# Moving one row of a modulation gradient into the last stage, its products to ScalarE, and a few gradient products to other places

## The chip, the cores and the metric

The kernel runs on one core of a Trainium2 chip. The time is device time in microseconds (us) from the start of the program to its end, outputs written. Three runs before took 1404.22, 1406.06 and 1412.09 us (median 1406.06).

## What is computed

One transformer-like block and its gradient, in bf16, for S = 2048 tokens of D = 1024 features and an MLP width of F = 3584. Cut to what matters:

```python
mod = (silu(c) @ w_mod)              # six rows of 1024: sa, ca, ga, sb, cb, gb
h = layernorm(x) * (1 + ca) + sa
x = x + ga * irfft2(rfft2(h) * (w_r + 1j * w_i))
h = layernorm(x) * (1 + cb) + sb
out = x + gb * (gelu(h @ w1 + b1) @ w2 + b2)
# returned: out, and the gradients of x, w_r, w_i, w1, b1, w2, b2, c and w_mod for grad_out
```

The Fourier transforms are done as matrix products with cosine and sine matrices. The gradient of `w_mod` is an outer product of u = silu(c) (1024 values) with the gradient of `mod` (6 rows of 1024), so it is 1024 x 6144. The gradient of `c` needs, for each of the six rows, `w_mod[:, row] * gradient row` summed along the row.

## The kernel before

The kernel keeps TensorE (PE) fed with large products of 16 matmuls (128x512 each, accumulated in one PSUM tile). Two families of such products are independent of almost everything else and are used as filling between the steps of the backward Fourier transform: 56 **gw2 products** (gradient of w2, line 1289, copied out of PSUM by ScalarE, line 1297, or by any engine in the first eight blocks) and 56 **gw1 products** (gradient of w1, line 1550, copied out by ScalarE at line 1554). `pieces()` is a Python generator that emits one product for each step; `fill(n)` (line 1562) emits the next n. Both families take their PSUM tile from a pool of four (`ps_f`), so PE can be at most four products ahead of the copies.

Each engine executes its own list of instructions in order. A scheduler makes these lists when the kernel is built, from the order in which the Python code issues the operations, from priorities (`tc.high_priority()` around the copies out of PSUM) and from `tc.issue_after(ins)`, which puts what is issued under it behind the instruction `ins`. DMAs are issued by SP (plain loads, stores and transposing loads), by POOL (scattered loads and stores, the stores of the gradients of w1 and w_mod) and by ScalarE's queue (the store of each late gw2 half row, line 1298). A queue that waits to issue one DMA also holds those behind it.

The stages from about 975 us on, which the change touches:

- **Pair stage** (`spectral_core(False, ...)`, the eight steps of the loop over `par` and `m`). Each step multiplies a slice of the transform by the filter and makes the filter's gradient (VectorE, DVE, line 195), with four gw2 products as filling (`beside_bwd`, line 1589). The transposed `hh` operand of each gw2 block is loaded by SP (lines 1507 and 1509) into a ring of three buffers. Between the products `beside_bwd` also runs 17 steps of `gmod_ring` (line 1185) for **rows 3 and 4** of w_mod: SP loads 256 KB of w_mod (line 1190), DVE multiplies and sums it (line 1201), DVE makes the product `u * gradient row` (line 1203) and POOL stores it (line 1204). The steps are given out as 2, 3, 3, 3, 3, 3, 0, 0 to the eight pairs. Two inverse transforms (`s_inv`, line 652, copied out to `V` by ScalarE) come before the seventh pair.
- **Split inverse**: for the classes CO and SO `half_class` (line 1422) makes the inverse in halves (line 1431), with one `fill(1)` behind CO; then 24 small groups `po` (line 775) for four blocks of tokens, with `fill(1)` at some places of the loop over `npp` (line 765).
- **Token blocks**: `consume_bwd` (line 1460) is called for i = 0 to 3. It undoes the folds on DVE, normalizes on ScalarE (line 518), runs `scaled_rows` (line 1252) and `ln_bwd` (line 1242: a product and sum on DVE at line 1244, a scaled copy on ScalarE at line 1246, an addition on DVE), loads `d_gx1` (line 1476), adds and stores with `store_tok` (line 165 on SP, the scattered half at line 167 on POOL). It fills with 3, 7, 7, 8 products, then column sums on PE (`accCA`), then 2, 2, 1, 2.
- **Last stage** (line 1608): `gmod_row` for rows 5, 2, 1, 0. Each of its eight steps (`gmod_steps`, line 1172) loads 256 KB of w_mod on SP into a ring of four (`wrw`, line 1176), makes the product on DVE into a ring of four (part of `otl`, line 1177), stores it from POOL (line 1178) and multiplies and sums on DVE (line 1179). Beside it run the remaining 27 gw1 products, six behind each row.

Of the kernel before, what the change touches and what calls it, by code (L numbers as in the profile page):

```python
# [13 lines left out]
ACT = mybir.ActivationFunctionType  # L14
ALU = mybir.AluOpType
# [20 lines left out]
def kernel(  # L36
# [24 lines left out]
    nc = tc.nc  # L61
    CE, CO, SE, SO = 0, 1, 2, 3
# [131 lines left out]
    def tt(out, a, b, op):  # L194
        return nc.vector.tensor_tensor(out=out, in0=a, in1=b, op=op)  # L195
# [188 lines left out]
    for j in range(4):  # L384
        for cch in range(NDC):
            pt = ps_f("pt")
            for a in range(4):
                q = (0, 2, 3, 1)[a] if j % 2 == 0 else (1, 3, 2, 0)[a]
# [159 lines left out]
    def spectral_core(fwd, fb, sms, em, css, pt, evac_u, evac_c, evac_v, consume, o4tag, pfs=None, fill=lambda n: None, mid=lambda: None, beside=lambda n, r_in: None):  # L548
# [156 lines left out]
        for par in range(2):  # L705
            for m in range(4):
# [14 lines left out]
                if par == 0 and m > 0:  # L721
# [6 lines left out]
                    else:  # L728
                        cl = (CE, SE)[m - 2]
# [4 lines left out]
        for cl in (CO, SO):  # L734
            if fwd:
                s_inv_half(cl, smis[1], 0)
                continue
            Vs[cl] = reg.tile([P, 8, 512], BF16, name=f"V{cl}", tag=f"uv{cl}")

            def r_cols(c8, i, cl=cl):  # L740
                dc = c8 // 2
                base = (0, 1, 2, 1)[dc] + 256 * (c8 % 2) + (PW if (dc >= 2) == (cl < 2) else 0)
                return R[:, cl * 4 + i, :, :].rearrange("p x w -> p (x w)")[:, base:base + 255:2]

            half_class(cl, Vs[cl], r_cols, evac_v)
            if cl == CO:
                fill(1)
        with tc.issue_after(r_in[0].ins):
            nc.vector.tensor_scalar(out=gm[:, 8:12, :], in0=gm[:, 4:8, :], scalar1=-1.0, scalar2=None, op0=ALU.mult)
        xts = [reg.tile([P, 4, D], BF16, name="xt", tag="sma")[:]]  # L750
# [6 lines left out]
        for i in range(4):  # L757
            if fwd and i == 0:
                tmp, eb, o4 = first
            else:  # L760
                o4, on, tmp = ct[:, 3 * (i % 2)], ct[:, 3 - 3 * (i % 2)], ct[:, 1 + i % 2]
                if fwd and i == 2:
                    eb = tmp
            half = [(cl, eb[:, 2 * k + cl // 2], k * 256 + i // 2 * P) for cl in (CE, SE) for k in range(2)]
            for npp, (cl, ov4, c0) in enumerate((half if i % 2 == 0 else []) + [(cl, o4[:, cl], i * P) for cl in (CO, SO)]):
                if npp in (2, 4):
                    fill(1)
                for hh_ in range(2):
                    npo[0] += 1
                    po = ((ps_d, ps_s) if fwd else (ps_d, ps_s, ps_d, ps_f))[npo[0] % (2 if fwd else 4)]("po")  # L770
                    for d2 in range(2):
                        dc = 2 * hh_ + d2
                        for h in range(2):
                            gi = 2 * dc + h + (4 if (dc >= 2 and cl >= 2) else 0)
                            nc.tensor.matmul(po[:, d2 * 256:(d2 + 1) * 256], lhsT=Vs[cl][:, 2 * dc + h, c0:c0 + P],
                                             rhs=gm[:, gi, :], start=(h == 0), stop=(h == 1))
                    with tc.high_priority():
                        ov = ov4[:, hh_ * 512:(hh_ + 1) * 512]
                        if fwd or (cl, hh_) != (3, 0):
                            nc.any.tensor_copy(out=ov, in_=po[:])  # L780
                        else:
                            last_po[0] = nc.scalar.copy(out=ov, in_=po[:])
            if i % 2 == 0:
                tt(o4[:, 0:4:2, :], eb[:, 0:2, :], eb[:, 2:4, :], ALU.add)
                if fwd and i == 2:
                    tt(on[:, 0:4:2, :], eb[:, 0:2, :], eb[:, 2:4, :], ALU.subtract)
            elif not fwd or i == 1:
                tt(o4[:, 0:4:2, :], eb[:, 0:2, :], eb[:, 2:4, :], ALU.subtract)
            if i == 0:
                if fwd:  # L790
                    for cl in (CO, SO):
                        s_inv_half(cl, smis[1], 1)
                    ct = reg.tile([P, 4, 4, D], BF16, name="ct", tag=o4tag)
                xts.append(reg.tile([P, 4, D], BF16, name="xt", tag="smb" if fwd else "px0")[:])
            consume(i, o4, tmp, ct[:, 2 - i % 2], xts[i % 2], eb)
# [376 lines left out]
    def gmod_steps(r, wrs, gws, gr):  # L1172
        nc.sync.dma_start(out=gr, in_=d_gmod[r * D:(r + 1) * D].partition_broadcast(P))
        for jc in range(NDC):
            wr, gw = wrs[:, jc % wrs.shape[1], :], gws[:, jc % gws.shape[1], :]
            nc.sync.dma_start(out=wr, in_=w_mod[jc * P:(jc + 1) * P, r * D:(r + 1) * D])
            nc.vector.tensor_scalar(out=gw, in0=gr, scalar1=u_rt[:, jc:jc + 1], scalar2=None, op0=ALU.mult)
            nc.gpsimd.dma_start(out=out_9[jc * P:(jc + 1) * P, r * D:(r + 1) * D], in_=gw)
            nc.vector.tensor_tensor_reduce(out=wr, in0=wr, in1=gr, scale=1.0, scalar=0.0,
                                           op0=ALU.mult, op1=ALU.add, accum_out=gu[:, r, jc:jc + 1])  # L1180
            yield
# [57 lines left out]
    def ln_sums(gs):  # L1239
        nc.vector.tensor_scalar(out=gs, in0=gs, scalar1=-1.0 / D, scalar2=None, op0=ALU.mult)  # L1240

    def ln_bwd(g, gsum, n_ap, tmp):
        sc = small.tile([P, 1], FP32, tag="lbsc", bufs=4)
        nc.vector.tensor_tensor_reduce(out=tmp, in0=g, in1=n_ap, scale=-1.0 / D, scalar=0.0,  # L1244
                                       op0=ALU.mult, op1=ALU.add, accum_out=sc[:])
        nc.scalar.activation(out=tmp, in_=n_ap, func=ACT.Identity, scale=sc[:], bias=gsum)  # L1246
        tt(g, g, tmp, ALU.add)

    def scaled_rows(out4, in4, row, gs, r, b):
# [201 lines left out]
    sacc = otl[:, 2 * NT * P:2 * NT * P + D]  # L1451
# [8 lines left out]
    def consume_bwd(i, o4, tmp, tmp2, n1, eb):  # L1460
        if i == 0:
            accCA.append(ps_s("accCA"))
            nc.vector.tensor_copy(out=sacc, in_=eb[:, 0, :])
        elif i == 2:
            tt(sacc, sacc, eb[:, 0, :], ALU.add)
        unfold_d(o4, tmp)
        unfold_tok(o4, tmp)
        load_tok(n1, A_x, i, nc.gpsimd)
        with tc.issue_after(last_po[0].ins):
            norm_act(n1, n1, 0, i)  # L1470
        tt(tmp, o4, n1, ALU.mult)
        s1c = small.tile([P, 4], FP32, tag="s1c")
        scaled_rows(o4, o4, opca_row, s1c, 0, i)
        for q in range(4):
            ln_bwd(o4[:, q, :], s1c[:, q:q + 1], n1[:, q, :], tmp2[:, q, :])
        nc.sync.dma_start(out=n1, in_=chunk_rows(d_gx1, i))
        tt(o4, o4, n1, ALU.add)
        store_tok(out_1, o4, i)
        fill((3, 7, 7, 8)[i])
        halves_sum(accCA[0], tmp, i == 0, i == 3)  # L1480
        fill(1 if i == 2 else 2)
        if i == 3:
            rows = small.tile([P, D], BF16, tag="gmrow", bufs=1)
            store_halves(accCA[0], rows[0:64, 0:KH], tmp, 1)
# [13 lines left out]

    def gmod_row(r, ins):
        with tc.issue_after(ins.ins):  # L1500
            for _ in gmod_steps(r, w1g["wr"], w1g["gw"], w1g["gr"][:, r % 2, :]):
                pass

    def pieces():
# [36 lines left out]
        for fg in range(F // 512):  # L1541
            if fg == 3:
                w1g["gz"] += [reg.tile([P, 8, 512], BF16, name=f"gzu{k}", tag=f"uv{k}") for k in range(4)]
            for k in {0: (1,), 1: (2,), 2: (3,), 3: (4, 5, 6)}.get(fg, ()):
                w1g["ins"] = gw1_load(k)
            gz2 = w1g["gz"][2 * w1g["set"][fg]:2 * w1g["set"][fg] + 2]
            for cch in range(NDC):
                acc = ps_f("gw1acc")
                for t in range(NT):
                    nc.tensor.matmul(acc[:], lhsT=n3ns[t // 4][:, t % 4, cch * P:(cch + 1) * P], rhs=gz2[t // 8][:, t % 8, :],  # L1550
                                     start=(t == 0), stop=(t == NT - 1))
                ob = gwo1[:, (fg * NDC + cch) % 8]
                with tc.high_priority():
                    nc.scalar.copy(out=ob, in_=acc[:])  # L1554
                eng = nc.sync if fg == 6 and cch > 4 else nc.gpsimd
                eng.dma_start(out=out_4[cch * P:(cch + 1) * P, fg * 512:(fg + 1) * 512], in_=ob)  # L1556
                yield
# [4 lines left out]
    def fill(n):  # L1562
        for _ in range(n):
            next(todo)
        done[0] += n
# [18 lines left out]
        for step in step_in[3:8]:  # L1584
            behind(step, ins)

    rows34 = gmod_ring((3, 4), gmy, sacc)

    def beside_bwd(n, r_in):
        for k in range(4):  # L1590
            fill(1)
            if 3 - k < (2, 3, 3, 3, 3, 3, 0, 0)[n]:
                with tc.issue_after(hh_in[0].ins), tc.issue_after(r_in.ins) if n == 7 else ExitStack():
                    next(rows34)

    spectral_core(False, fbuf2, (smA2, None), em2, [css2[:, 0], css2[:, 1]],
                  new_pair_temps(["t0", "t1", "t2", "t3"]), s_copy, s_copy, s_copy, consume_bwd, "fr", pfs, fill, mid_bwd, beside_bwd)
# [7 lines left out]
    unfold_d(sr[0:1, 0], sr[0:1, 1])  # L1605
    store_gmod([sr[0:1, 0, 0, 0:KH], sr[0:1, 0, 0, KH:D]], 0)

    for r in (5, 2, 1, 0):
        gmod_row(r, w1g["ins"])
        fill(6)  # L1610
    fill(NFC * 4 - done[0])
    fin2 = reg.tile([P, 2, P], BF16, name="fin2", tag="gm")
    make_identity(nc, fin2[:, 0, :])
# [40 lines left out]
```

## Time and profile before

| | us |
|---|---|
| runs: lowest, median, highest | 1404.22, 1406.06, 1412.09 |
| the profiled execution's own time | 1412.43 |
| its span, first to last instruction | 1410.7 |
| TensorE busy in it | 1354.3 |
| VectorE busy | 1066.7 |
| ScalarE busy | 759.4 |

The profile is of one execution. An engine's busy time says how long its instructions ran; a row of a timeline gives start, length, engine, line and operation, `out<-in` by the program's names, how many instructions were merged (x16), and in brackets how long the engine sat idle before it and what ended that wait. PE is TensorE's matmul row, DVE is VectorE, ACT ScalarE, POOL GpSimd, SPq and ACTq the queues that issue DMAs. L1550 is line 1550 of the kernel before.

### The profile page before, as it was taken

What the parts mean: (1) busy time and instruction counts of PE and PEld (TensorE: products, weight loads), DVE (VectorE), ACT (ScalarE), POOL (GpSimd) and SP (SyncE); (2) the same over time, 40 slices, a digit from 0 to 9 for tenths busy, and PEclk for the clock granted to TensorE, in tenths of its full rate; (3) what the DMA queues carried; (4) which work ended last, traced back from release to release, by engine and by line L of the source; (5) the groups of instructions that cost most, each with busy time, mean ns of one, the idle gap of its engine ahead of it and who ended that gap; (6) DMA issues with size and microseconds to landing.
All of it is one profiled execution on the core that took longest, in us unless ns stands there. A gap on an engine that the chain in (4) does not pass through costs nothing. (4 is left out here: it accounts for less than half of the span.)

```text
span 1410.7 us, 18467 instructions
## 1 busy us (share of the span) xinstructions
PE 1354.3 (96%) x6774; PEld 658.6 (47%) x6899; DVE 1066.7 (76%) x1479; ACT 759.4 (54%) x1082; POOL 355.4 (25%) x434
## 2 busy tenths in 40 slices
PE   5898999999999999999999999999999899999998
PEld 2445565444444444444444444444644455444444
DVE  5897889977888787887620678889686778968781
ACT  4775657657967766665314593443622454534311
POOL 5410523201212122112211011011254420322542
PEclk8999999999999999999999999999999999999999
DMA  9972746799787777696999499995499987798993
GB/s 318 282 235 61 199 138 194 253 294 351 255 253 230 235 239 243 192 296 224 287 276 272 119 255 308 257 263 148 123 287 262 262 195 204 218 257 171 282 338 111
DMA packets 360689, 331.12 MB, mean 235 GB/s; under 512 B 207962, under 2 KB 303088, under 8 KB 360470
## 3 DMA queue, kind: packets, MB, share of 16 engines
q1 hardware_dynamic: 319702, 204.96, 55.8%
q0 software_dynamic: 35136, 119.73, 24.1%
q10 hardware_dynamic: 5760, 5.25, 1.2%
q8 instruction: 54, 0.88, 0.3%
q14 instruction: 37, 0.30, 0.1%
HBM read 165.73 MB, written 114.87 MB: 199 GB/s over the span
## 5 line engine op out<-in xcount | busy, mean ns | idle before, releaser
L840 PE MATMUL pp<-gBoT,wt 128*128 128x512 bf16 x874 | 196.5, 380 | 4.3 <-ACT phr L846 1.9
L1131 PE MATMUL pg<-w1T,gzr 128*128 128x512 bf16 x877 | 194.3, 379 | 1.3 <-issue 0.5
L1550 PE MATMUL gw1acc<-gzh,n3n 128*128 128x512 bf16 x627 | 139.1, 379 | 3.8 <-ACT gwo L1554 3.1
L1550 PEld LDWEIGHTS <-n3n 128*128 128x128 bf16 x896 | 87.4, 98 | 108.7 <-issue 5.0
L840 PEld LDWEIGHTS <-wt 128*128 128x128 bf16 x896 | 87.6, 98 | 107.9 <-issue 6.4
L1131 PEld LDWEIGHTS <-gzr 128*128 128x128 bf16 x896 | 86.6, 98 | 108.4 <-issue 5.8
L977 PEld LDWEIGHTS <-w 128*128 128x128 bf16 x896 | 87.2, 98 | 106.9 <-issue 2.5
L977 PE MATMUL pz<-n3Tb,w 128*128 128x512 bf16 x437 | 98.4, 379 | 1.7 <-DVE w2sD L1053 1.0
L977 PE MATMUL pz<-n3Ta,w 128*128 128x512 bf16 x439 | 98.0, 379 | 0.4
L1289 PE MATMUL gw2acc<-gB,hhsA 128*128 128x512 bf16 x405 | 93.1, 384 | 5.1 <-DMA hhsA<-d_hhT 4.5
L195 DVE TENSOR_TENSOR ct<-ct 128x2048 bf16<-128x2048 bf16 (+1 forms) x84 | 91.5, 1117 | 7.6 <-DMA d_n<-ct 3.7
L1031 PEld LDWEIGHTS <-hhA 128*128 128x128 bf16 x608 | 59.0, 98 | 72.8 <-issue 2.6
L980 ACT ACTIVATE gt<-pz,b_col 128x512 bf16<-128x512 f32 x112 | 72.8, 683 | 33.3 <-PE pz L977 33.0
L988 ACT ACTIVATE gt<-gt 128x2048 bf16<-128x2048 bf16 x28 | 53.5, 1911 | 64.5 <-DVE gt L195 64.5
L1554 ACT CAST gwo<-gw1acc 128x512 bf16<-128x512 f32 x56 | 31.9, 582 | 98.5 <-PE gw1acc L1550 70.9
L195 DVE TENSOR_TENSOR gt<-gt,gt 128x2048 bf16<-128x2048 bf16 x56 | 68.5, 1224 | 19.8 <-ACT gt L990 18.5
L1297 ACT CAST gwo<-gw2acc 128x512 bf16<-128x512 f32 x40 | 23.5, 586 | 96.0 <-PE gw2acc L1289 72.7
L1289 PEld LDWEIGHTS <-hhsA 128*128 128x128 bf16 x416 | 40.8, 99 | 53.7 <-DMA hhsA<-d_hhT 5.1
L1556 POOL DMA_DIRECT2D out_dram<-gwo x53 | 29.4, 556 | 107.3 <-ACT gwo L1554 107.0
L1550 PE MATMUL gw1acc<-gzu,n3n 128*128 128x512 bf16 x250 | 55.1, 379 | 0.3
L984 ACT ACTIVATE gt<-gt 128x2048 bf16<-128x2048 bf16 x28 | 53.5, 1910 | 2.3 <-DVE hhC L195 1.6
L990 ACT ACTIVATE gt<-gt 128x2048 bf16<-128x2048 bf16 x28 | 53.4, 1907 | 0.4
(366 smaller groups left out, 2535.8 us busy)
## 6 DMA issues: line engine op xcount, KB each, us to landing
gzr<-d_gz SPq DMA_DIRECT2D x28, 512.0 KB
wblk<-in_w_mod_dram SPq DMA_DIRECT2D x12, 1024.0 KB
out_dram<-otl POOLq DMA_DIRECT2D x48, 256.0 KB, 4.8
d_ph<-pho POOLq DMA_DIRECT2D x21, 512.0 KB, 5.6
d_hh<-hhA POOLq DMA_DIRECT2D x19, 512.0 KB, 5.0
wrw<-in_w_mod_dram SPq DMA_DIRECT2D x32, 256.0 KB
w<-in_B_w_dram SPq DMA_DIRECT2D x7, 1024.0 KB
hhC<-d_ph SPq DMA_DIRECT2D x14, 512.0 KB
```

The source lines that it names most:

```text
L195: return nc.vector.tensor_tensor(out=out, in0=a, in1=b, op=op)
L840: last_pe[0] = nc.tensor.matmul(pp[:], lhsT=wt[:, fc % 4, cch, :], rhs=gBoT[j][:, cch, :], start=(cch == 0), stop=(cch == NDC - 1))
L977: last_pe[0] = nc.tensor.matmul(pz[:], lhsT=w1s[g][:, cch, k * P:(k + 1) * P], rhs=n3T[:, cch, :], start=(cch == 0), stop=(cch == NDC - 1))
L980: z_in = nc.scalar.activation(out=zb[:, k, :], in_=pz[:], func=ACT.Identity, bias=b1_col[:, fc:fc + 1], scale=1.0)
L984: nc.scalar.activation(out=av, in_=zb, func=ACT.Square)
L988: nc.scalar.activation(out=sg, in_=bv, func=ACT.Sigmoid, scale=2.0 * GK)
L990: nc.scalar.activation(out=bv, in_=bv, func=ACT.Sigmoid, scale=-2.0 * GK)
L1031: last_pe[0] = nc.tensor.matmul(pbs[i][:], lhsT=hh[:, k, i * P:(i + 1) * P], rhs=wp[:, k, :], start=False, stop=(g == 6 and k == 3))
L1131: last_pg[0] = nc.tensor.matmul(pgs[i][:], lhsT=gzs[b, g][:, k, i * P:(i + 1) * P], rhs=w1Ts[g][:, k, h * KH:(h + 1) * KH], start=(g == 0 ...
L1289: nc.tensor.matmul(acc[:], lhsT=hh_of(fc)[:, t, :], rhs=gBs[t // 4][:, t % 4, h * KH:(h + 1) * KH], start=(t == 0), stop=(t == NT - 1))
L1550: nc.tensor.matmul(acc[:], lhsT=n3ns[t // 4][:, t % 4, cch * P:(cch + 1) * P], rhs=gz2[t // 8][:, t % 8, :], start=(t == 0), stop=(t == NT ...
L1554: nc.scalar.copy(out=ob, in_=acc[:])
```

## The change

Five edits, all behind 975 us:

1. `gmod_ring` handles row 3 alone. Its nine steps are given out as 1, 1, 2, 2, 2, 1, 0, 0 instead of seventeen.
2. Row 4 becomes a `gmod_row` of the last stage, which now runs rows 5, 4, 2, 1, 0, with five products behind each instead of six. The two buffers of the gradient row alternate accordingly.
3. In the last stage the products of rows above 1 (5, 4 and 2) are made on ScalarE; those of rows 1 and 0 stay on DVE.
4. The split inverse has a `fill(1)` behind SO as well as behind CO; in exchange the first one between the `po` groups of token block 0 is left out. In `consume_bwd` six of the products are issued ahead of `scaled_rows` for i > 0, and the counts become 0, 6, 6, 6 ahead, then 4, 1, 2, 2 and 1, 2, 1, 2. Token block 2 has nine products instead of eight, so 26 instead of 27 are left for the last stage.
5. For i > 0 the scaled copy of `ln_bwd` on ScalarE is issued behind the latest gw1 copy out of PSUM, which at that place is the sixth of the block.

```diff
             half_class(cl, Vs[cl], r_cols, evac_v)
-            if cl == CO:
-                fill(1)
+            fill(1)
...
-                if npp in (2, 4):
+                if npp in (2, 4) and (fwd or (i, npp) != (0, 2)):
                     fill(1)
...
             nc.sync.dma_start(out=wr, in_=w_mod[jc * P:(jc + 1) * P, r * D:(r + 1) * D])
-            nc.vector.tensor_scalar(out=gw, in0=gr, scalar1=u_rt[:, jc:jc + 1], scalar2=None, op0=ALU.mult)
+            if r > 1:
+                nc.scalar.activation(out=gw, in_=gr, func=ACT.Identity, scale=u_rt[:, jc:jc + 1])
+            else:
+                nc.vector.tensor_scalar(out=gw, in0=gr, scalar1=u_rt[:, jc:jc + 1], scalar2=None, op0=ALU.mult)
...
-    def ln_bwd(g, gsum, n_ap, tmp):
+    def ln_bwd(g, gsum, n_ap, tmp, order=ExitStack):
...
-        nc.scalar.activation(out=tmp, in_=n_ap, func=ACT.Identity, scale=sc[:], bias=gsum)
+        with order():
+            nc.scalar.activation(out=tmp, in_=n_ap, func=ACT.Identity, scale=sc[:], bias=gsum)
...
         tt(tmp, o4, n1, ALU.mult)
+        fill(6 if i else 0)
...
-            ln_bwd(o4[:, q, :], s1c[:, q:q + 1], n1[:, q, :], tmp2[:, q, :])
+            ln_bwd(o4[:, q, :], s1c[:, q:q + 1], n1[:, q, :], tmp2[:, q, :],
+                   (lambda: tc.issue_after(w1g["ev"].ins)) if i else ExitStack)
...
-        fill((3, 7, 7, 8)[i])
+        fill((4, 1, 2, 2)[i])
         halves_sum(accCA[0], tmp, i == 0, i == 3)
-        fill(1 if i == 2 else 2)
+        fill((1, 2, 1, 2)[i])
...
-            for _ in gmod_steps(r, w1g["wr"], w1g["gw"], w1g["gr"][:, r % 2, :]):
+            for _ in gmod_steps(r, w1g["wr"], w1g["gw"], w1g["gr"][:, (r + (r > 3)) % 2, :]):
...
-                    nc.scalar.copy(out=ob, in_=acc[:])
+                    w1g["ev"] = nc.scalar.copy(out=ob, in_=acc[:])
...
-    rows34 = gmod_ring((3, 4), gmy, sacc)
+    row3 = gmod_ring((3,), gmy, sacc)
...
-            if 3 - k < (2, 3, 3, 3, 3, 3, 0, 0)[n]:
+            if 3 - k < (1, 1, 2, 2, 2, 1, 0, 0)[n]:
                 with tc.issue_after(hh_in[0].ins), tc.issue_after(r_in.ins) if n == 7 else ExitStack():
-                    next(rows34)
+                    next(row3)
...
-    for r in (5, 2, 1, 0):
+    for r in (5, 4, 2, 1, 0):
         gmod_row(r, w1g["ins"])
-        fill(6)
+        fill(5)
     fill(NFC * 4 - done[0])
```

In the built program the ScalarE list of the last stage has the 24 products in groups between the copies out of PSUM: two products behind the last `ln_bwd` copy of block 3, a copy, three products, a copy, three products, a copy, the two scalings `sr`, and from there three products before each copy until the twenty-fourth. POOL's list has the store of each product in the same order; the two scattered stores of block 3 (line 167) stand between the stores of the sixth and the seventh product.

## The prediction

> **What bounds the kernel now.** First the page's busy times.
>
> ```profile
> span 1410.7 us, 18467 instructions
> ...
> PE 1354.3 (96%) x6774; PEld 658.6 (47%) x6899; DVE 1066.7 (76%) x1479; ACT 759.4 (54%) x1082; POOL 355.4 (25%) x434
> ```
>
> TensorE (PE) is the bound. The change removes none of its products, so what it can win are PE's idle times from 970 us on. The waits of PE from 970 to the end:
>
> ```profile
> PE gw2acc L1289 <- DMA hhsA<-d_hhT: 4.5, 2, 2.9
> PE gw1acc L1550 <- ACT gwo L1554: 3.1, 2, 1.9
> PE pv L652 <- ACT V L807: 2.9, 1, 2.9
> PE pu L1431 <- ACT smbf L807: 2.0, 3, 0.9
> PE accCA L218 <- DVE ct L195: 1.1, 1, 1.1
> ```
>
> 13.6 us in all. PE's timeline gives their places (in brackets the idle time ahead of a row), and the last stage, where PE has none.
>
> ```profile
> 1077.81 7.08 PE L1289 MATMUL gw2acc<-gB,hhsA 128*128 128x512 bf16 x31 [1.68 <-DMA hhsA<-d_hhT]
> ...
> 1091.63 1.91 PE L581 MATMUL pcs<-empf,U 128*128 128x256 bf16 x16
> 1096.41 15.60 PE L1289 MATMUL gw2acc<-gB,hhsA 128*128 128x512 bf16 x63 [2.87 <-DMA hhsA<-d_hhT]
> 1111.84 1.91 PE L652 MATMUL pv<-smf,R 128*128 128x256 bf16 x16
> 1116.60 7.07 PE L652 MATMUL pv<-smf,R 128*128 128x256 bf16 x48 [2.85 <-ACT V L807]
> ...
> 1167.63 1.91 PE L775 MATMUL po<-gm,V 128*128 128x256 bf16 x16
> 1193.11 0.61 PE L218 MATMUL accCA<-ct,ones_bf 128*32 128x512 bf16 x8 [1.09 <-DVE ct L195]
> 1275.89 27.83 PE L1550 MATMUL gw1acc<-gzh,n3n 128*128 128x512 bf16 x125 [1.22 <-ACT gwo L1554]
> 1309.69 3.61 PE L1550 MATMUL gw1acc<-gzh,n3n 128*128 128x512 bf16 x16 [1.87 <-ACT gwo L1554]
> 1313.57 10.52 PE L1550 MATMUL gw1acc<-gzh,n3n 128*128 128x512 bf16 x48
> 1323.93 55.42 PE L1550 MATMUL gw1acc<-gzu,n3n 128*128 128x512 bf16 x250
> 1379.19 27.79 PE L1550 MATMUL gw1acc<-gzh,n3n 128*128 128x512 bf16 x126
> ```
>
> From 1323.93 to 1379.19 PE does 256 matmuls (250 recorded): 55.26 us, so 3.45 us for a product of 16. The last row ends at 1406.98; what follows PE to the span's end is 3.7 us.
>
> **Pair stage: fewer steps for the ring.** Eight of seventeen steps leave SP's and DVE's lists there: eight loads, sums, products and stores.
>
> ```profile
> SPq L1190 <- DMA out_dram<-otl: 33.1, 9, 9.7
> ```
>
> SP waited 33.1 us at the ring's loads for stores to free a buffer, and the hhsA loads stand behind these on SP. With half the steps that wait goes, and with it the 1.68 and the 2.87. A gap can also cost clock; the windows of 1095 to 1100, 1115 to 1120 and 1305 to 1310 us (the granted clock is the third number from the end):
>
> ```profile
> 1095.00:1100.00 5.00, 3.59 (x10) 1.29 (x11) 4.93 (x8) 0.75 (x2) 1.45 (x3) 0.66 1.06 267
> 1115.00:1120.00 5.00, 3.40 (x17) 2.48 (x17) 5.00 (x9) 4.11 (x8) 2.81 (x3) 0.68 1.13 277
> 1305.00:1310.00 5.00, 3.13 (x16) 1.36 (x14) 5.00 (x10) 3.99 (x4) 0.07 (x1) 1.00 1.08 235
> ```
>
> Behind the 2.87 the 64 matmuls to 1111.84 took 15.43 us for 13.80: 1.6 lost. Behind the 2.85 the 48 half-width ones took 6.91 for 5.2: 1.7 lost. Behind the 1.87, nothing. All that this stage can return is 1.68 + 2.87 + 1.6 + 2.85 + 1.7 = 10.7 us.
>
> The Trainium skill (TensorE: Matmul & The Clock Gate, Part 1: The HAM clock gate) has the clock halve only behind idle windows of about 3.4 us. By that no clock would return here and the 10.7 would be 7.4; the trace differs, 2.85 us of idling sufficed.
>
> But what is late next? The V copy, for which PE waited at 1116.60:
>
> ```profile
> 1115.48 0.58 ACT L1297 CAST gwo<-gw2acc 128x512 bf16<-128x512 f32 x1 [6.30 <-DMA otl<-d_hh]
> 1115.96 3.04 ACT L807 CAST V<-pv 128x512 bf16<-128x512 f32 x6
> ```
>
> ```profile
> 1101.89 1.22 DVE L1201 CUSTOM_DVE_ANT_0 otl<-otl 128x1024 bf16<-128x1024 bf16 x1
> 1105.38 0.48 DVE L1203 TENSOR_SCALAR otl<-otl,u_rt 128x1024 bf16<-128x1024 bf16 x1
> ```
>
> ```profile
> 1107.53 3.52 SPq L1509 DMA_TRANSPOSE otl<-d_hh  x1
> ```
>
> ScalarE idled 6.30 us for the transposing load, issued at 1107.53 behind the filter-gradient stores of the pair, which DVE feeds. The chain from `pcs` (1091.63) through DVE, SP, this load and ScalarE to V (1115.96) takes 24.3 us. The change takes one sum and one product out of it, 1.2 + 0.4 = 1.6 by these two rows. If `pcs` comes 4.5 us earlier and V only 1.6 + 1.7 (the first gap lies ahead of the chain), PE waits there instead. I take 1.7 + 1.5 = **−3.2 us**; the bounds are 0 (another load takes the place) and −10.7.
>
> **accCA.** Four products stand ahead of it, where PE had three and a half: the 1.09 goes, **−1.1** (bounds 0, −1.1).
>
> **Split inverse.** The products behind SO and ahead of `po` change places. PE had no wait between SO and the row of 1167.63: 0; the 2.0 at `pu` stays.
>
> **Copies behind the sixth copy.** ScalarE before:
>
> ```profile
> 1272.99 2.37 ACT L1246 ACTIVATE ct<-xt,s1c,sc 128x1024 bf16<-128x1024 bf16 x2 [10.42 <-DVE s1c L1240]
> ...
> 1305.65 3.52 ACT L1246 ACTIVATE ct<-xt,s1c,sc 128x1024 bf16<-128x1024 bf16 x3 [11.63 <-DVE s1c L1240]
> 1309.08 0.56 ACT L1554 CAST gwo<-gw1acc 128x512 bf16<-128x512 f32 x1
> ```
>
> It sat 10.42 and 11.63 us at a layer norm copy that waited for DVE, with a finished product behind it; PE ran out of PSUM tiles. With six copies ahead of that point both waits go, 1.22 + 1.87 = **−3.1** (all, or nothing). The ninth product in block 2 is one fewer at the end: 0 in sum. Without any wait in the last stage PE would end at 1406.98 − 3.1 = 1403.9; the eleventh product of block 3 would start at 1313.57 − 3.1 + 3.45 = 1313.9, the fifteenth at 1327.7.
>
> **Row 4 and the products on ScalarE.** Block 3 and the last stage before, DVE, POOL, the DMAs, SP and ScalarE:
>
> ```profile
> 1315.25 1.28 DVE L1177 TENSOR_SCALAR otl<-gr,u_rt 128x1024 bf16<-128x1024 bf16 x3 [3.00 <-DMA gr<-d_gmod]
> ...
> 1323.27 2.27 DVE L195 TENSOR_TENSOR ct<-ct,xt 128x4096 bf16<-128x4096 bf16 x1
> ```
>
> ```profile
> 1214.95 1.73 POOL L167 DMA_INDIRECT out_dram<-ct,xu  x1 [2.37 <-DVE ct L195]
> 1216.98 1.02 POOL L167 DMA_INDIRECT out_dram<-ct,xu  x1 [0.30 <-issue]
> ...
> 1325.82 5.58 POOL L167 DMA_INDIRECT out_dram<-ct,xu  x1 [2.24 <-DVE ct L195]
> 1331.70 2.43 POOL L167 DMA_INDIRECT out_dram<-ct,xu  x1 [0.30 <-issue]
> ```
>
> ```profile
> L1178 POOL DMA_DIRECT2D out_dram<-otl x32 | 17.5, 547 | 30.9 <-DVE otl L1177 30.7 <-issue 0.2
> ```
>
> ```profile
> out_dram<-otl POOLq DMA_DIRECT2D x32, 256.0 KB, 4.7
> ```
>
> ```profile
> 1309.94 0.57 SPq L1173 DMA_DIRECT2D gr<-d_gmod  x1
> ```
>
> Before, the products were on DVE and a late buffer stopped only DVE. Now ScalarE's list has three products ahead of each gw1 copy, so a product that waits for a buffer holds the copy, and behind four copies PE. A product should cost what the layer norm copy of the same shape does, 3.52 / 3 = 1.17, 3 x 1.17 + 0.56 = 4.1 with a copy: over PE's 3.45 by itself. Products take a ring of four buffers: the n-th waits for the store of the (n−4)-th to land, a turn of 1.17 + 0.55 + 4.7 = 6.4 us, 1.6 for each product, 4.8 for three.
>
> And one store comes late. On POOL the seventh product's store stands behind the two scattered stores of line 167, which wait for DVE's last addition of block 3. DVE's list now has six sums ahead of the additions: from the landing of gr (1315.25) six of the 1.22 that such a sum takes (row of 1101.89), 7.3, then four additions of about 0.6 (2.27 for one merged row) and the wait for POOL of 2.24: 1327.2. The two scattered stores take 3.1 (1214.95 to 1218.0) or 8.3 (1325.82 to 1334.1); I take the 3.1, nearer to a POOL without a backlog. The seventh store leaves at 1330.3 + 0.5, lands 4.7 later at 1335.5; the eleventh product, which reuses its buffer, ends at 1336.7, the eleventh copy at 1337.2. The fifteenth product on PE needs that copy's PSUM tile: 1337.2 for 1327.7, **9.5 us late**. PE's clock falls behind such a gap (1.6 as above). The ScalarE list goes on with three products before each copy to the fifteenth copy (23 products), so copies 12 to 15 come at 4.8 each: 1342.0, 1346.8, 1351.6, 1356.4. PE's sixteenth product is ready at 1337.2 + 3.45 + 1.6 = 1342.25 and needn't wait; the next three wait 1.1, 1.35 and 1.35. PE ends at 1403.9 + 9.5 + 1.6 + 3.8 = 1418.8, **+11.9 against 1406.98**, the 3.1 of the copies already in it. The bound below is ScalarE's own pace, with no store late: 23 products, eight copies and the two `sr` scalings (1.06) from 1315.2 on put the fifteenth copy at 1315.2 + 26.9 + 4.5 + 1.1 = 1347.7, where PE without a wait wants to start its nineteenth product at 1341.5: 6.2 late, +3.1 against 1406.98. The bound above has the scattered stores at 8.3: 5.2 more, +17.1. The 11.9 is what the rows make of it with the two prices that I chose, 3.1 and 4.7.
>
> DVE loses 24 products and gains a row's eight sums. Behind 1327.2 it has 34 sums of 1.22 and 16 products of 0.48, 49 us, to 1376 if nothing starves it; there are 43 us to spare before PE ends, so what follows PE keeps its 3.7 (a cost of 0; if the sums ended last, the end would move with them).
>
> **Sum.** −3.2 − 1.1 + 11.9 = +7.6, on the profiled execution's 1412.43 (its span of 1410.7 and 1.7 around it): 1420.0. That execution is 6.4 above the median of the runs shown; on the median 1406.06 the same +7.6 gives **1413.7**.
>
> **Rivals.** *B, faster:* the transposing load lands ahead of PE and the pair stage returns its 10.7, accCA 1.1, and in the last stage a store lands so soon that ScalarE's own pace is all, +3.1: −8.7, 1397.4. It decides where the seventh product's store lands by about 1326 and the load for V some 3 us before PE is there. For it: the first wait is gone with the ring's steps, and half of the ring's transfers leave the pair stage. Against it: 4.7 us as the median of 32 stores, and the chain of 24.3 us, which is mostly not the ring's. The Trainium skill (DMA: Bandwidth & Descriptors, Anatomy of one DMA — SWDGE (gpsimd) path) fits 2.0 us and bytes over 436e3 to such a DMA: an estimate of 2.6 us for 256 KB, by which a turn of the ring would be 4.3 us, three products 3.2, and ScalarE's own pace the limit, as in B. The trace's 4.7 speaks against it. *C, slower by more:* the scattered stores take their 8.3 us, so the seventh store lands at 1340.7 and the last stage costs 17.1: −3.2 − 1.1 + 17.1 = +12.8, 1418.9; with nothing from the pair stage either, 1422. For it: the 8.3 is this very pair of stores in before. Against it: the pair at 1214.95 took 3.1. *D:* the change doesn't do what it says. The built lists show every move, so only the split inverse is left, and it gives nothing in the sum; it gets no chance.
>
> **How the numbers follow.** A (the sum) 0.58, B 0.22, C 0.20. About 0.5%, 7.0 us, is what a measurement here can tell from no change: faster is below 1399.0, slower above 1413.1. Within A the last stage may lie half way to either bound (4.4 less or 2.6 more) and the pair stage may return 0 to 5: 1407.5 to 1419.5, none of its chance below, 0.27 within and 0.31 above; B 0.15 below and 0.07 within; C 0.20 above: 0.15, 0.34, 0.51. The range takes all of C and leaves out half of B: 1398 to 1422.
>
> **What would show it.** Right: PE without the hhsA waits in the pair stage but still with one at `pv` for V; no wait for gwo in blocks 2 and 3; about 1327 one long wait of PE for gwo, while ScalarE waits at a product for a store of otl and POOL for DVE's `ct`. Wrong: no gap of PE behind 1310, or stores of products that land in 3 us (B); no wait at `pv`; gr much later than 1315; a product on ScalarE far from 1.17 us; DVE's sums so late that they end behind PE. A wrong step in the last stage moves the result more than all others together.

## The result and the profile after

| | before | after |
|---|---|---|
| median of 12 runs each (us) | 1405.99 | 1412.99 |
| lowest and highest | 1401.11, 1412.09 | 1407.51, 1418.89 |
| the profiled execution's own time | 1412.43 | 1410.80 |
| its span | 1410.7 | 1408.9 |
| TensorE's waits from 970 us on, in the profile, all of them | 14.0 | 14.1 |

The ratio of after to before is 1.0049, with a 95% interval of 1.0029 to 1.0068: 7.0 us slower where 7.6 were forecast (1413.7 for 1412.99). The two profiled executions lie the other way round, by 1.6 us, and part of that stays open below. (The prediction's 13.6 for the waits left out two of 0.2.) So the sum came out; the first question is whether its terms did.

PE's waits in the changed kernel, from 970 us to the end:

```profile
PE gw1acc L1555 <- ACT gwo L1559: 13.1, 4, 8.1
PE pu L1434 <- ACT smbf L806: 0.8, 2, 0.6
...
```

Every wait of more than 0.2 us that stood in this list before is gone but the one at `pu`: no hhsA, no V, no accCA. All that PE waits now is for gw1 copies, and its timeline says where (line numbers are five higher than before):

```profile
1087.30 1.91 PE L581 MATMUL pcs<-empf,U 128*128 128x256 bf16 x16
1089.05 13.98 PE L1292 MATMUL gw2acc<-gB,hhsA 128*128 128x512 bf16 x64
1102.86 7.26 PE L652 MATMUL pv<-smf,R 128*128 128x256 bf16 x64
...
1261.80 27.79 PE L1555 MATMUL gw1acc<-gzh,n3n 128*128 128x512 bf16 x128
1289.52 0.61 PE L218 MATMUL accCA<-ct,ones_bf 128*32 128x512 bf16 x8
...
1297.42 7.07 PE L1555 MATMUL gw1acc<-gzh,n3n 128*128 128x512 bf16 x32
1304.33 3.62 PE L1555 MATMUL gw1acc<-gzu,n3n 128*128 128x512 bf16 x16
1310.44 5.30 PE L1555 MATMUL gw1acc<-gzu,n3n 128*128 128x512 bf16 x16 [2.49 <-ACT gwo L1559]
1323.88 12.95 PE L1555 MATMUL gw1acc<-gzu,n3n 128*128 128x512 bf16 x48 [8.14 <-ACT gwo L1559]
1338.13 3.61 PE L1555 MATMUL gw1acc<-gzu,n3n 128*128 128x512 bf16 x16 [1.30 <-ACT gwo L1559]
1342.93 34.69 PE L1555 MATMUL gw1acc<-gzu,n3n 128*128 128x512 bf16 x160 [1.19 <-ACT gwo L1559]
```

From `pcs` to `pv` PE runs through without a gap. Behind 1304 it has four gaps of 13.1 us, and two of the rows behind a gap are long: 5.30 where a row of one product takes 3.62, 12.95 where a row of three takes 10.52 (before, at 1313.57): 4.1 us, with a granted clock of 0.68 in the first and 0.60 in the first 6 us of the second. The row of 1297.42 holds the eleventh and twelfth product of block 3, so the row of 1323.88 starts with the fifteenth, the one that the prediction named.

What ScalarE did in these gaps, from its timeline:

```profile
1302.67 2.39 ACT L1177 ACTIVATE otl<-gr,u_rt 128x1024 bf16<-128x1024 bf16 x2
1308.77 1.15 ACT L1177 ACTIVATE otl<-gr,u_rt 128x1024 bf16<-128x1024 bf16 x1 [3.71 <-DMA out_dram<-otl]
1309.82 0.56 ACT L1559 CAST gwo<-gw1acc 128x512 bf16<-128x512 f32 x1
1311.86 1.06 ACT L1609 ACTIVATE sr<-accSA 1x512 f32<-1x512 f32 x2 [1.47 <-issue]
1312.83 2.17 ACT L1177 ACTIVATE otl<-gr,u_rt 128x1024 bf16<-128x1024 bf16 x2
1322.21 1.15 ACT L1177 ACTIVATE otl<-gr,u_rt 128x1024 bf16<-128x1024 bf16 x1 [7.21 <-DMA out_dram<-otl]
1323.27 0.56 ACT L1559 CAST gwo<-gw1acc 128x512 bf16<-128x512 f32 x1
```

POOL, which issues the stores:

```profile
1304.12 0.54 POOL L1180 DMA_DIRECT2D out_dram<-otl  x1 [0.51 <-ACT otl L1177]
1312.06 1.74 POOL L167 DMA_INDIRECT out_dram<-ct,xu  x1 [7.40 <-DVE ct L195]
1314.11 1.98 POOL L167 DMA_INDIRECT out_dram<-ct,xu  x1 [0.30 <-issue]
1316.09 0.59 POOL L1180 DMA_DIRECT2D out_dram<-otl  x1
```

DVE, whose last addition of block 3 POOL waits for:

```profile
1304.65 1.20 DVE L1181 CUSTOM_DVE_ANT_0 wrw<-wrw,gr 128x1024 bf16<-128x1024 bf16 x1
...
1309.49 2.29 DVE L195 TENSOR_TENSOR ct<-ct,xt 128x4096 bf16<-128x4096 bf16 x1 [3.63 <-DMA xt<-d_gx]
```

Read from below: the addition waits 3.63 us for the load of d_gx1, POOL 7.40 for the addition, the seventh product's store leaves at 1316.09, and the eleventh product on ScalarE, which takes its buffer, starts at 1322.21: that store landed 6.0 us after its issue. The copy behind it frees the tile for the row of 1323.88. The shorter gap of 2.49 us has another store at its start: the eighth product waited 3.71 us for the store of the fourth, issued at 1300.80, which took 7.9 us to land.

To compare the kernels part by part, the table takes four starts on PE from each profile: `pcs` of the fourth pair, accCA of block 1, accCA of block 3 and the last transpose (`ptr`). From the fourth pair to accCA of block 1 all have the same products. From there to accCA of block 3 those with the moved products have one more (3.45 us), behind it one fewer.

| profile | start of pcs | to accCA 1 | to accCA 3 | to ptr |
|---|---|---|---|---|
| before | 1058.66 | 166.20 | 78.78 | 103.27 |
| before, second profile (e1) | 1059.16 | 163.92 | 82.18 | 102.93 |
| after | 1056.18 | 152.53 | 80.81 | 115.66 |
| after, second profile (e12) | 1059.45 | 152.08 | 82.25 | 114.08 |

From the fourth pair to accCA of block 1 the changed kernel takes 11 to 14 us less, in the last stage 11 to 13 us more in spite of its one product less. That is the whole change: two large terms of opposite sign.

### The profile page after: what moved, and what is told of

Its sections match the earlier page's. It is cut to its first block, busy times and chain, and to the rows that moved or that the text cites. A ratio compares the mean times of both kernels' runs of the same rounds, so it can differ in the third digit from the quotient of the medians.

```text
span 1408.9 us, 18603 instructions
## 1 busy us (share of the span) xinstructions
PE 1362.2 (97%) x6899; PEld 655.5 (47%) x6899; DVE 1057.9 (75%) x1455; ACT 784.3 (56%) x1106; POOL 347.2 (25%) x434
## 5 line engine op out<-in xcount | busy, mean ns | idle before, releaser
L987 ACT ACTIVATE gt<-gt 128x2048 bf16<-128x2048 bf16 x28 | 53.5, 1911 | 64.5 <-DVE gt L195 64.5
L1555 PE MATMUL gw1acc<-gzu,n3n 128*128 128x512 bf16 x256 | 60.2, 399 | 13.1 <-ACT gwo L1559 13.1
L1181 DVE CUSTOM_DVE_ANT_0 wrw<-wrw,gr 128x1024 bf16<-128x1024 bf16 x40 | 48.0, 1215 | 9.2 <-DMA wrw<-in_w_mod_dram 9.2
L983 ACT ACTIVATE gt<-gt 128x2048 bf16<-128x2048 bf16 x28 | 53.5, 1909 | 2.3 <-DVE hhC L195 1.6
```

The costliest lines, as they stand in the source:

```text
L983: nc.scalar.activation(out=av, in_=zb, func=ACT.Square)
L987: nc.scalar.activation(out=sg, in_=bv, func=ACT.Sigmoid, scale=2.0 * GK)
```

## Experiments

Each ratio is to the kernel before in the same set, whose median was 1410.6 in the first four, 1411.75 in the next four and 1411.96 in the last four; the changed kernel itself was timed beside a median of 1405.99. So ratios from two sets are less sure against each other than inside one, and the stage times of the profiles stand beside them ("the last stretch" is the last column of that table).

**e1: the kernel before, again.**

> The kernel before, a second profile. The changed kernel's profile shows the whole 10.7 us of the pair stage and the 1.1 of accCA gone, and yet the median rose by 7.0. Theory T1: the profiled execution of before (1412.43, 6.4 above its median) was not typical, and an ordinary one has less idle time of PE in the pair stage: a time near 1406 and waits there of 3 to 5 us instead of 7.4. Rival R1: the waits are the same 7.4 us, and the 6 us lie ahead of 970 us (a slower start).

One run: 1413.72 us. PE's waits:

```profile
PE gw1acc L1550 <- ACT gwo L1554: 4.3, 2, 3.0
PE pv L652 <- ACT V L807: 3.6, 1, 3.6
PE gw2acc L1289 <- DMA hhsA<-d_hhT: 2.5, 1, 2.5
```

The pair stage waits at two of its three places, 6.1 us for 7.4. That fits neither T1's 3 to 5 nor R1's 7.4. Of the two waits for gwo one (2.98 us, at 1275.86) is again at the layer norm copies of block 2; the other (1.31, at 1328.67) isn't at those of block 3 but behind the two `sr` scalings of the last stage, which had waited 13.10 us on ScalarE for DVE's last addition. The execution was again above its set's median. What an ordinary execution of before does without is not seen.

**e2: all products of the last stage on DVE.**

```diff
-            if r > 1:
+            if r > 9:
                 nc.scalar.activation(out=gw, in_=gr, func=ACT.Identity, scale=u_rt[:, jc:jc + 1])
```

> The changed kernel with all products of the last stage back on DVE. Theory T2: the last stage's gaps come from products on ScalarE that wait for a buffer ahead of a copy; without them PE has no wait for gwo behind 1300 us, 12 to 13 us come back, and the time is 1412.99 - 12 = about 1401 (1397 to 1403). Rival R2: it is the eight more steps of row 4 in this stage (DVE's sums, the stores behind the scattered ones) that cost; then PE still waits there, or DVE ends behind PE, and the time stays within 3 us of 1413.

Ratio 0.9897 (0.9876 to 0.9918). All of PE's waits from 970 us on:

```profile
PE pu L1434 <- ACT smbf L806: 1.0, 3, 0.6
PE pcs L581 <- ACT smbf L806: 0.2, 1, 0.2
```

No wait for gwo is left, and from accCA of block 3 to the end PE takes 97.78 us, 17.9 less than after the change. The eight steps of row 4 cost PE nothing here; R2 falls. The gain is larger than expected: 1.0049 to 0.9897 is 1.5%, 21 us, but across two sets; by the profiles it is the 17.9, or 16.3 with the changed kernel's second profile (e12). This is also the best kernel of the study, 1.0% faster than before, since it keeps what the other edits win.

**e3: the ring for row 3 alone, row 4 left out.**

```diff
-    rows34 = gmod_ring((3, 4), gmy, sacc)
+    rows34 = gmod_ring((3,), gmy, sacc)
+    nc.gpsimd.memset(gu[:, 4, :], 0.0)
...
-            if 3 - k < (2, 3, 3, 3, 3, 3, 0, 0)[n]:
+            if 3 - k < (1, 1, 2, 2, 2, 1, 0, 0)[n]:
```

> The kernel before with the ring for row 3 alone; row 4 is left out altogether (its part of the w_mod gradient isn't written and its part of the gradient of c is zero), all else as before. It prices the pair stage. T1: an ordinary execution has 3 to 6 us to return: 1400 to 1403. R1: the whole 10.7 returns, 1395. By the prediction's working (only 3.2, the V copy next): a wait of PE at pv of about 5 us stays and the time is 1402.8.

Ratio 0.9937 (0.9921 to 0.9954), 8.9 us (6.5 to 11.1). PE's waits:

```profile
PE gw1acc L1550 <- ACT gwo L1554: 3.1, 2, 1.8
PE accCA L218 <- DVE ct L195: 0.7, 1, 0.7
...
```

The wait at `pv` that the prediction kept isn't there. To accCA of block 1 PE takes 152.20, as in the changed kernel, 14.0 and 11.7 less than in the two profiles of before. The prediction's working of the pair stage falls; by time the gain lies between T1 and R1, and R1's 10.7 is inside the interval. The run takes out the loads, sums, products and stores of eight steps together, so it doesn't tell waits in the lists from lighter DMA traffic.

**e4: the moved products and the later layer norm copies alone (edits 4 and 5).**

```diff
-            if cl == CO:
-                fill(1)
+            fill(1)
...
-                if npp in (2, 4):
+                if npp in (2, 4) and (fwd or (i, npp) != (0, 2)):
...
+        fill(6 if i else 0)
...
-            ln_bwd(o4[:, q, :], s1c[:, q:q + 1], n1[:, q, :], tmp2[:, q, :])
+            ln_bwd(o4[:, q, :], s1c[:, q:q + 1], n1[:, q, :], tmp2[:, q, :],
+                   (lambda: tc.issue_after(w1g["ev"].ins)) if i else ExitStack)
...
-        fill((3, 7, 7, 8)[i])
+        fill((4, 1, 2, 2)[i])
...
-        fill(1 if i == 2 else 2)
+        fill((1, 2, 1, 2)[i])
```

> The kernel before with the moved products and the layer norm copies behind the sixth copy alone (edits 4 and 5). Theory T3: the two waits for gwo of 1.2 and 1.9 us and the one at accCA go, 4.2 in all: about 1402. Rival R3: the waits go but come back at the layer norm, whose copies are now later (PE waits at accCA or po instead): 1405 to 1407.

Ratio 0.9972 (0.9955 to 0.9989), 3.9 us. Neither accCA nor gwo is in PE's waits, and the last stretch takes 97.78, the same as in e2. T3 holds, with the size that it gave. The pair stage, untouched here, still has its waits: 5.5 us at `pv` and 3.5 for hhsA.

**e5: the scattered stores of block 3 behind row 1's products.**

```diff
+        if r == 1:
+            with tc.issue_after(w1g["st"].ins):
+                scatter_tok(out_1, w1g["o4"], 3)
```

`w1g["st"]` is the latest store of a product, `scatter_tok` the two scattered stores taken out of `store_tok` for block 3.

> The changed kernel with the two scattered stores of block 3 issued behind the stores of row 1's products. Theory T2a: ScalarE's products stall because the seventh product's store stands behind those two stores on POOL; then the waits of PE of 2.5 and 8.1 us and the 4.5 us of clock behind them go, the two of 1.2 and 1.3 stay at most: 1.2% less than the changed kernel, ratio to before about 0.993 (0.990 to 0.996). Rival R2a: the ring's own turn (store to land, 4.4 us) or ScalarE's pace holds PE: ratio over 1.000.

Ratio 0.9997 (0.9981 to 1.0014). ScalarE's waits from 1290 to 1345 us in the changed kernel:

```profile
ACT otl L1177 <- DMA out_dram<-otl: 14.8, 8, 7.2
...
ACT sr L1609 <- issue: 1.5, 1, 1.5
```

and in e5:

```profile
ACT otl L1182 <- DMA out_dram<-otl: 10.9, 11, 2.2
...
ACT sr L1615 <- issue: 0.6, 1, 0.6
```

The long wait of 7.2 is gone, as the late store was to give, but eleven short ones take its place: the products wait for the turn of their four buffers. The last stretch takes 109.15, 11.4 over e2's. T2a as the only cause falls; by the last stretch R2a carries more than half. In this profile one wait at a layer norm copy of block 2 was back as well:

```profile
1269.97 29.12 PE L1561 MATMUL gw1acc<-gzh,n3n 128*128 128x512 bf16 x128 [3.70 <-ACT gwo L1565]
```

**e6: block 3's load of d_gx1 ahead of the fifth w_mod load of row 5.**

```diff
+            with tc.issue_after(w1g["gx"].ins) if r == 5 and jc > 3 else ExitStack():
-            nc.sync.dma_start(out=wr, in_=w_mod[jc * P:(jc + 1) * P, r * D:(r + 1) * D])
+                nc.sync.dma_start(out=wr, in_=w_mod[jc * P:(jc + 1) * P, r * D:(r + 1) * D])
```

> The changed kernel with block 3's d_gx1 load on SP ahead of the fifth to eighth w_mod load of row 5, where it stood behind the sixth. In the changed kernel's profile DVE's last addition waited 3.6 us for this load. T2a with the load as its start: the scattered stores leave some 3 to 5 us sooner and the 8.1 us gap shrinks as much: ratio 1.000 to 1.002. Rival: DVE's sums, which now wait for later w_mod loads, take the load's place: ratio 1.004 to 1.006, no change.

Ratio 1.0001 (0.9985 to 1.0018). PE's longest wait is 4.8 us instead of 8.1, and the last stretch 112.31 for 115.66 and 114.08. The chain starts at the load, as T2a has it, for 1.8 to 3.4 us.

**e7: only row 5's products on ScalarE.**

```diff
-            if r > 1:
+            if r > 4:
                 nc.scalar.activation(out=gw, in_=gr, func=ACT.Identity, scale=u_rt[:, jc:jc + 1])
```

> The changed kernel with only row 5's products on ScalarE, rows 4 and 2 on DVE. T2a: the products that wait for the late stores are those from the eleventh on, now on DVE, where they hold no copy; at most the 2.5 us wait of PE stays: ratio 0.990 to 0.992 (all on DVE gave 0.9897). Rival R2a (each product on ScalarE costs alike): a third of the 1.5% between all on ScalarE and all on DVE: 0.995.

Ratio 0.9931 (0.9913 to 0.9949), between the two answers. The last stretch takes 100.9: eight products on ScalarE cost 3.1, twenty-four cost 17.9. In this profile too PE waited 2.0 us in block 2, a wait that e2's profile doesn't have.

**e8: the early load and the late scattered stores together (the edits of e5 and e6).**

> The early load of d_gx1 and the late scattered stores together, products as in the changed kernel. T2a: once the scattered stores are out of the way, the load no longer matters: within 0.002 of the late scattered stores alone. Rival (the load holds DVE's sums, and these hold the stage): 0.003 or more below it.

Ratio 0.9988 (0.9971 to 1.0005), 0.0009 below e5: the load doesn't matter once the scattered stores are away. The last stretch stays at 110.46.

**e9: six buffers for the products, scattered stores late (e5's edit and this one).**

```diff
-            wr, gw = wrs[:, jc % wrs.shape[1], :], gws[:, jc % gws.shape[1], :]
+            wr, gw = wrs[:, jc % wrs.shape[1], :], gws[:, w1g["n"] % 6, :]
+            w1g["n"] += 1
...
-        w1g["gw"] = otl[:, 0:4 * D].rearrange("p (a d) -> p a d", d=D)
+        w1g["n"] = 0
+        w1g["gw"] = otl[:, 0:6 * D].rearrange("p (a d) -> p a d", d=D)
```

> The changed kernel with the two scattered stores late, and the products' ring of four buffers made six. In the run with late scattered stores alone ScalarE's 24 products took 43.4 us (1303.5 to 1346.9), 1.8 each, and the ratio stayed at 1.000. Theory T4: the ring's own turn, product, issue and landing over four buffers, makes that pace; with six it falls to ScalarE's own (24 x 1.05, nine copies at 0.5 and 1.0 for the scalings: 31 us), PE waits 0 to 3 us, ratio 0.990 to 0.993. Rival R4: the w_mod loads, DVE's sums or the DMA rate hold it: ratio 0.997 or more.

Ratio 0.9964 (0.9946 to 0.9983), between T4 and R4. ScalarE's waits:

```profile
ACT sr L1617 <- DVE ct L200: 5.9, 1, 5.9
...
ACT otl L1183 <- DMA out_dram<-otl: 2.8, 2, 2.0
```

The ring's waits fall from 10.9 to 2.8, as T4 has it, though the stores land no sooner: the median of the last stage's 40 is 5.3 us here, 4.8 in e5 and 4.4 in the changed kernel. But ScalarE, now early, runs into a third hold: the two `sr` scalings, which stand in its list behind eight products and wait for DVE's last addition of block 3.

```profile
1317.67 9.19 PE L1563 MATMUL gw1acc<-gzu,n3n 128*128 128x512 bf16 x32 [5.09 <-ACT gwo L1567]
1327.88 41.89 PE L1563 MATMUL gw1acc<-gzu,n3n 128*128 128x512 bf16 x192 [1.02 <-ACT gwo L1567]
```

PE's first wait is that one. The last stretch takes 106.61, still 8.8 over e2's.

**e10: six buffers, scattered stores in their place (e9's edit without e5's).**

> The changed kernel with six buffers for the products, scattered stores in their old place. T4 with the late store beside it: the seventh store is late as before, but now holds the thirteenth product, not the eleventh, so PE still has one wait of 2 to 6 us: ratio 0.994 to 0.999. If the late store alone were the cause, six buffers would bring two products' worth, 2 to 3 us: 1.003.

Ratio 1.0014 (0.9994 to 1.0035), outside T4's range and nearer to the late store's. ScalarE:

```profile
ACT otl L1178 <- DMA out_dram<-otl: 7.6, 2, 6.0
...
ACT sr L1611 <- DVE ct L195: 4.8, 1, 4.8
```

Two waits in a row: 4.8 at the scalings, then 6.0 at the thirteenth product for the seventh one's store. The last stretch is 111.83.

**e11: three buffers.**

```diff
-            wr, gw = wrs[:, jc % wrs.shape[1], :], gws[:, jc % gws.shape[1], :]
+            wr, gw = wrs[:, jc % wrs.shape[1], :], gws[:, w1g["n"] % 3, :]
+            w1g["n"] += 1
```

> The changed kernel with three buffers for the products. T4: each product takes a third of the turn, not a quarter: 1.8 x 4 / 3 = 2.4 us, 24 x 0.6 = 14 us more, of which the late store covers some: ratio 1.011 to 1.017. If the late store alone were the cause: the tenth product waits, not the eleventh: 1.006 to 1.008.

Ratio 1.0071 (1.0046 to 1.0096), below T4's 1.011, in the range of the late store alone; by ratio it isn't clear of the changed kernel's 1.0049, by the last stretch (119.08) it is 3.4 to 5.0 us longer. The products' waits for a buffer grew from 14.8 to 21.9 us:

```profile
ACT otl L1178 <- DMA out_dram<-otl: 21.9, 12, 6.3
```

The late store and the smaller ring overlap: the late store covers most of the 14 us that T4 gave the smaller ring.

**e12: the changed kernel, again.**

> The changed kernel, a second profile. The first execution had 13.1 us of waits for gwo behind 1300 us and lay 2.2 below the median. Theory T5: the last stage varies with the landing of its loads and stores, and the pair stage stays without waits; the wait at the last stage differs by some us from 13.1, in the direction of the time. Rival: the front ahead of 970 us makes the difference.

One run: 1413.47 us.

```profile
PE gw1acc L1555 <- ACT gwo L1559: 14.4, 5, 8.9
```

Five waits of 14.4 for four of 13.1. But the fifth isn't in the last stage; it is at the layer norm copies of block 2, where edit 5 was to leave none:

```profile
1266.06 27.79 PE L1555 MATMUL gw1acc<-gzh,n3n 128*128 128x512 bf16 x128 [1.28 <-ACT gwo L1559]
```

The four of the last stage sum to 13.1 in both profiles, and the last stretch is 1.6 shorter for less clock lost. Of the 2.7 us between the two profiles 3.3 lie ahead of 970 us and 1.4 between accCA of blocks 1 and 3, and the other stretches give 2.0 back. So the rival holds for most of the difference, T5's varying last stage doesn't; its other half does, the pair stage has no wait in either.

## Why the prediction came out, point by point

**The sum was right by luck: two of its terms were not, and their errors cancelled.** The predicted terms, what the profiles show and what the timed runs show:

| step | predicted | in the profiles | by time |
|---|---|---|---|
| pair stage and accCA | −4.3 | −11.4 to −14.1 (after and e12 against before and e1) | −8.9 (e3, the pair stage alone) |
| layer norm copies | −3.1 | −3.1 and −3.0 (the waits there in before and e1); 1.3 is left in e12 | −3.9 (e4, with accCA) |
| last stage, against PE without waits | +15.0 | +17.9 and +16.3 (115.66 and 114.08 against 97.78) | +21 (after against e2, across two sets) |

The first two by time make −12.8, and e2, which has both and no product on ScalarE, measured −14.5 in the same set (0.9897 of 1410.6). The third by time is only the difference of e2 and the result, so it checks nothing on its own. With it the time went as forecast because the pair stage gave back about 6 us more and the last stage took about 6 us more than forecast. By the prediction's own list "no wait at `pv`" was a sign of being wrong, and it came.

**Pair stage: the step that failed.** The prediction had V's copy late next, at the end of a chain of 24.3 us from the `pcs` of 1091.63, since "the change takes one sum and one product out of it". The changed kernel shows what that missed:

```profile
1084.28 0.53 SPq L1192 DMA_DIRECT2D otl<-in_w_mod_dram  x1
1084.91 0.89 SPq L634 DMA_DIRECT2D out_dram<-smf  x2
1085.96 0.35 SPq L565 DMA_DIRECT2D empf<-d_P  x1
1087.50 5.11 SPq L1514 DMA_TRANSPOSE otl<-d_hh  x1
```

The transposing load that ScalarE waited for is issued 0.2 us behind the start of `pcs` (1087.30), where before it came 15.9 us behind it (1107.53 for 1091.63). On SP the load stands in both kernels behind the stores of one pair's filter gradient (`smf`), which DVE makes. That pair is not the one of 1091.63 but the one before it, whose `pcs` started at 1074.22 and whose copies ScalarE began at 1078.91; so the chain doesn't run through the `pcs` from which the prediction counted it. In before, DVE came to that pair's first operation (`Pt`) only at 1095.93, since it stood 7.37 us at a ring's sum right ahead of it:

```profile
1094.26 1.23 DVE L1201 CUSTOM_DVE_ANT_0 otl<-otl 128x1024 bf16<-128x1024 bf16 x1 [7.37 <-DMA otl<-in_w_mod_dram]
```

```profile
1078.91 2.56 ACT L807 CAST cs01b<-pcs 128x512 bf16<-128x512 f32 x4
1095.93 1.29 DVE L195 TENSOR_TENSOR Pt<-cs01b 128x1028 bf16<-128x1028 bf16 x2
```

In the changed kernel the same operation waits for ScalarE's copy and for nothing of the ring:

```profile
1075.02 1.30 DVE L195 TENSOR_TENSOR Pt<-cs01b 128x1028 bf16<-128x1028 bf16 x2 [1.16 <-ACT cs01b L806]
```

I counted the durations of what left DVE's list, 1.6 us, and not the waits that left with it. Rival B's half of the story was the right one here: in the profiles all 10.7 came back, and e3 shows it with the other edits left out (8.9 by time). That the waits did it, and not the lighter DMA traffic, is read from these rows; no run parts the two.

**accCA and the copies** went as worked out, apart from block 2: the wait there is gone in after, e2 and e4 but stands in other profiles of the same list, at 0.6 us in e8 and e10, 1.3 in e12, 2.0 in e7 and 3.7 in e5. In e5, e7 and e12 ScalarE sat 11.75, 10.03 and 9.33 us at the layer norm copy for DVE's sum, in after 6.73. So "all, or nothing" was too sharp.

**The last stage** went by the steps of the text, a few us later than each of them. Counted from the start of the eleventh product of block 3 (1313.9 on the prediction's clock, 1297.42 here):

| | predicted | measured |
|---|---|---|
| DVE's last addition ends | 13.3 | 14.4 |
| the seventh store leaves | 16.4 | 18.7 |
| the eleventh product on ScalarE ends | 22.8 | 25.9 |
| the fifteenth product on PE starts | 23.3 | 26.5 |

Two things differed in kind. The addition was late for the d_gx1 load (3.63 us), not only for the six sums: on SP that load, issued at 1300.27, stands behind two w_mod loads that wait for sums, a queue that the prediction didn't look at. That its 13.3 came near is luck too: it added 2.24 us, which in before POOL sat idle until the addition ended (1325.54; POOL starts at 1325.82) and which are no step of the chain. Without them the sum is 11.1, and the wait for the load is about the rest of the 14.4. And PE already waited 2.49 us at the fourteenth product, for the store of the fourth. The prices were near: a product on ScalarE 1.05 to 1.15 for 1.17, the scattered pair 4.0 (1312.06 to 1316.09) for 3.1, 4.4 as the median of the 40 stores of products for 4.7. But the stores that held PE took longer than the median, 7.9 and 6.0 us. The Trainium skill (DMA: Bandwidth & Descriptors, Anatomy of one DMA — SWDGE (gpsimd) path), whose fit gives an estimate of 2.6 for such a store, would by that have put the ring's turn under PE's pace; e5 with its eleven waits at the ring speaks against that.

**What holds the last stage is not one thing.** Shown by the runs: ScalarE's list has three holds ahead of gw1 copies, the ring's turn, the store behind the scattered stores, and the scalings behind DVE's last addition. They overlap, so one away shows the next. For a wait at the scalings the prediction had nothing. It was there before the change: `sr` waited 11.53 us in before, where PE lost nothing, and 13.10 in e1, where PE lost 1.31. Over e2's 97.78 the last stretch costs

| products on ScalarE, with | us |
|---|---|
| nothing else (after, e12) | 17.9, 16.3 |
| three buffers (e11) | 21.3 |
| d_gx1 early (e6) | 14.5 |
| six buffers (e10) | 14.1 |
| d_gx1 early and scattered stores late (e8) | 12.7 |
| scattered stores late (e5) | 11.4 |
| scattered stores late and six buffers (e9) | 8.8 |
| row 5 alone (e7) | 3.1 |

The prediction had put 9.5 of its 15 on the late store and the rest on the ring and the clock; the runs put 4.9 to 6.5 on the late store alone (e5 against e12 and after), 2.2 to 3.8 on the ring alone (e10) and 7.5 to 9.1 on both (e9). Of the 8.8 that e9 leaves, 7.2 are the wait at the scalings and the clock behind it (5.09 idle, then 9.19 for a row that takes 7.07 elsewhere). A kernel with all three holds out of the way and the products still on ScalarE wasn't tried; e2, which takes them off ScalarE, ends the matter more simply.

**What stays open.** In the profiles the terms sum to about nothing (1412.43 and 1413.72 before, 1410.80 and 1413.47 after), in 12 runs each to 7.0 us. Both profiled executions of before lie above the median of their set, by 6.4 and 3.1. An ordinary execution of before may lose less in the pair stage than these two, which e3's 8.9 by time against 11.7 and 14.0 by stage would fit; no trace of such an execution exists, so this is argued and not shown. There is a rival: before's median was 1405.99 beside the 12 runs of the changed kernel and 1410.6 to 1411.96 in the three later sets, where the changed kernel was run only once (e12, 1413.47, 1.5 above its set's median). How much of the 7.0 would stand in another set isn't known.

## What to carry to other kernels

When a step leaves an in-order queue, count the waits that it held as well as its length: ring steps with 1.6 us of DVE work on the prediction's chain had held a load back by 15.7 us, counted from `pcs`. Work that is moved to an engine which also empties PSUM must not be able to wait for a buffer or a store there: on DVE a wait of 3.05 us for such a buffer cost PE nothing (before, at 1322.26), on ScalarE one of 7.21 us stopped TensorE for 8.14 us. And where one hold is found, look in the same list for the next before giving it a price, since holds that overlap don't add up.

## What the runs showed of the hardware

What TensorE loses in clock behind a gap isn't set by the gap's length alone. In the changed kernel 2.49 us of idling were followed by a product of 5.30 us instead of 3.62, in e5 a gap of the same length by ten products at full speed (34.69 for 34.5). The granted clock (third number from the end) was 0.68 behind the first and 1.00 behind the second:

```profile
1310.44:1315.74 5.30, 5.30 (x16) 1.98 (x16) 5.30 (x9) 3.14 (x4) 3.38 (x2) 0.68 0.71 256
```

```profile
1345.92 34.69 PE L1561 MATMUL gw1acc<-gzu,n3n 128*128 128x512 bf16 x160 [2.49 <-ACT gwo L1565]
```

```profile
1345.92:1349.50 3.58, 3.58 (x17) 1.66 (x17) 3.58 (x8) 2.45 (x4) 1.39 (x3) 1.00 0.97 355
```

In e8 a longer gap, of 3.09 us, was followed by a product at 3.61, with the clock at 1.00 from 1321 to 1325:

```profile
1321.04 3.61 PE L1562 MATMUL gw1acc<-gzu,n3n 128*128 128x512 bf16 x16 [3.09 <-ACT gwo L1566]
```

The Trainium skill (TensorE: Matmul & The Clock Gate, Part 1: The HAM clock gate) counts idle time in free-running windows of about 3.4 us and has the clock halve after at least one idle window. By that neither gap of 2.49 us would cost clock, since both are shorter than one window; the 5.30 us at a granted clock of 0.68 behind the first differ from it, and the measurement decides.
